# Two unused 32-byte tiles that move on-chip tiles by 32 and 64 bytes in a retention and two-mixture kernel

## Chip, cores and metric

The kernel runs on one core of a Trainium2 chip. The metric is the device time of one execution in microseconds (us), the median of several runs. Engines are called as the profile calls them: PE (TensorE matmuls) and PEld (its weight loads), DVE (VectorE), ACT (ScalarE), POOL (GpSimd) and SP (SyncE, which issues nearly all DMAs).

## What is computed

Three stages follow each other; the output of one is the input of the next.

```python
# 1: retention, B=4, H=8, S=576, D=64
scores = q @ k.T / sqrt(D)
x = (scores * Dmat) @ v                  # Dmat[i, j] = gamma**(i-j) for i >= j, else 0
x = x.transpose(0, 2, 1, 3).reshape(2304, 512)
# 2: routed mixture, 8 experts of 512 -> 1024 -> 512: each row goes to its best expert
e = argmax(x @ w_gate);  x = gate * (relu(x @ w1[e]) @ w2[e])
# 3: dense mixture: every row goes through all 8 experts
P = exp(logits - logits.max())
for _ in range(8):                       # Sinkhorn
    P /= P.sum(1) + 1e-9;  P /= P.sum(0) + 1e-9;  P *= N / E
out = sum(P[:, e:e+1] * (relu(x @ w1[e]) @ w2[e]) for e in range(8))
```

## The kernel before

**Precision.** A float32 operand is split into a high part (rounded to the type `fp32r`) and a low part (the rest). A product is then three matmuls: high by high, high by low, low by high. ACT makes the high part by a cast, DVE the low part by a subtraction (`lo_of`, L239 to L240).

**Stages on the clock.** Retention and routing take about the first 100 us, the routed mixture lasts until about 378 us, Sinkhorn runs beside the first unit of the dense mixture until about 412 us, and the dense mixture fills the rest. It goes over the 2304 rows in three passes (`NP = 3`) of 768 rows, and in each pass over 8 experts.

**Dense mixture, features.** The rows of a pass are held transposed, in four quarters of [128, 2, 384] float32 (tiles `x`, L1074). A Strassen-like scheme makes seven combinations of them (the quarters themselves, and sums and differences, one of which needs a tile of its own, `t3`), and each is split into a high tile `ch` and a low tile `cl` of [128, 2, 384] (L1099 and L1100). These fourteen tiles are called the features here. In passes 2 and 3 the same places are filled again at L1551 (the trace calls them `ch`, `cl` in pass 2 and `c` in pass 3).

**Dense mixture, pass 1** (about 378 to 850 us) is written out in order: `unit` (L1302) issues per quarter of an expert seven `product`s (L1313) with weights in the `ring` tiles. A product is six matmuls of 384 columns, L1318 to L1320, with the weights standing in PE and a feature tile streamed past them. `second` (L1236) multiplies the hidden rows in `HH` and `HL` by the second weights, also in `ring`, in matmuls of 512 columns (L1248 to L1250). The split first weights are stored to DRAM (`w1s`, L1306) for the passes to come.

**Dense mixture, passes 2 and 3** (about 850 us to the end) are placed by a planner: every piece of work is a `Task` with an engine, a cost in us and what it waits for; PE's order is a fixed line of tasks, and the order on the other engines comes from due times in a small simulation. The planner knows costs and buffers, not addresses. `first_weights` (L1564) loads the split first weights from `w1s` into one of five tiles `wa` (L1572), and `chunk` (L1606) issues the six matmuls of a product, L1622 to L1624:

```python
for r in range(2):
    a, b = (w[:, k, o + 128 * r:o + 128 * (r + 1)] for k in range(2))                     # of a tile wa
    nc.tensor.matmul(ps, a, xh[:, r, :], start=first, ...)                              # L1622
    nc.tensor.matmul(ps, a, xl_[:, r, :], start=False, ...)                              # L1623
    nc.tensor.matmul(ps, b, xh[:, r, :], start=False, ...)                              # L1624
```

The hidden rows go to nine tiles `hq` and four tiles `hr`, which are one stock of buffers: which of them a task gets depends only on which is free. They are combined by DVE (L1510, L1513) and split by ACT (L1729) and DVE (L240) into tiles `sq`; the second weights go through the `raw` tiles (and the two halves of `sums`) into tiles `wb`. `chunk2` multiplies them, L1779 to L1781 in matmuls of 256 columns and, in pass 3, L1776 and L1777. DVE adds the results to the accumulators `a0` to `a5` and `ya0` to `ya2` (L1802).

**Routed mixture.** `flipped` (L738) does the same three matmuls as a product, L741 to L743: the weights stand in PE, from `ring` tiles, and the routed rows (`HH`, `HL`) or the hidden rows (`h`) are streamed, up to 384 columns.

**Where tiles lie.** Tiles are taken from pools in the order in which the code asks for them. A pool with `side="right"` is laid out from the upper end of the on-chip memory, under the right pools that are open then. The first right pool is `sums` (L80), so that everything in a later right pool lies under it: the tiles of the retention stage (`io`, `wk`, `st`), then the features (`xc`), then the small tables of the dense mixture (`sk`, L1062), then the accumulators (`acc`), then `wa`, `hq` and three small buffers (`early`, L1377). Tiles of the left pools (`raw`, `ring`, `HH`, `HL`, `h`, `sq`, `wb`, `hr`, `ya`) don't depend on them.

Of the kernel before, what the change touches and what calls it, by code (L numbers as in the profile page):

```python
# [7 lines left out]
F32 = mybir.dt.float32  # L8
# [28 lines left out]
def kernel(  # L37
# [41 lines left out]
    ringt[:3] = [ring_p.tile([128, 4096], F32R, name=f"ring{i}") for i in range(3)]  # L79
    sum_p = ctx.enter_context(tc.tile_pool(name="sums", bufs=1, side="right"))  # L80
    sumt = sum_p.tile([128, 1024], F32, name="sums")

    xs = dram.tile([N + 1, DM], F32, name="xs")
    lst = dram.tile([LIST, 1], I32, name="lst")
# [12 lines left out]
    def bank(i, shape=(128, 512)):  # L97
        return psum.tile(list(shape), F32, tag=f"b{i}", name=f"b{i}")
# [121 lines left out]
    def tick(us):  # L220
        clock["pe"] += us
# [839 lines left out]
    sk = ctx.enter_context(tc.tile_pool(name="sk", bufs=1, side="right"))  # L1061
# [2 lines left out]
    TP = NT // NP  # L1064
    GRP = TP * 64
    HT = TP // 2
    P = sk.tile([128, NT, E], F32, name="P")
    lgall = sk.tile([128, NT, E], F32, name="lgall")

# [137 lines left out]
    def sinkhorn():  # L1207
# [8 lines left out]
        nc.vector.tensor_scalar(lgall, lgall, m, None, ALU.subtract)  # L1216
        nc.scalar.activation(P, lgall, AF.Exp)
        for it in range(8):
            nc.vector.tensor_reduce(rs, P, AX.X, ALU.add)
            nc.vector.tensor_scalar(rs, rs, 1e-9, None, ALU.add)  # L1220
            nc.vector.reciprocal(ri, rs)
            nc.vector.tensor_tensor(P, P, ri.unsqueeze(2).to_broadcast([128, NT, E]), ALU.mult)
            nc.vector.tensor_reduce(ce, P.rearrange("p t e -> p e t"), AX.X, ALU.add)
            o = bank((yield), (128, 128))
            nc.tensor.matmul(o[:, 0:E], ones, ce, start=True, stop=True)
            nc.vector.tensor_scalar(cr, o[:, 0:E], 1e-9, float(E) / N, ALU.add, ALU.mult)
            nc.vector.reciprocal(cr, cr)
            nc.vector.tensor_tensor(P, P, cr.unsqueeze(1).to_broadcast([128, NT, E]), ALU.mult)
    for _ in steps:
# [7 lines left out]
    def second(u, rows_, half_f, tiles_, last):  # L1237
# [3 lines left out]
        for t in tiles_:  # L1241
            tick(0.648)
            s = slice((t % HT) * 128, (t % HT + 1) * 128)
            first = u["i"] == 0 and not last
# [9 lines left out]
    def finish(p, e, t, y):  # L1254
        if e == 0:
            ACC[t] = acc_p.tile([128, DM], F32, name=f"a{t}")
        a = ACC[t]
        sc = P[:, p * TP + t, e:e + 1]
        if p == 0 and e == 0:
# [38 lines left out]

    A = tuple(range(HT))
    Bt = tuple(range(HT, TP))  # L1300
    def unit(u, pre, mids):
# [760 lines left out]
```

## Time and profile before

| | us |
|---|---|
| median of 3 runs | 1803.58 (1803.28 to 1805.52) |
| the profiled execution's own time | 1805.65 |
| its span, first to last instruction | 1803.9 |

| engine | busy, us | share of the span | instructions |
|---|---|---|---|
| PE | 1780.9 | 99% | 11996 |
| PEld | 1686.3 | 93% | 11996 |
| DVE | 1235.2 | 68% | 2246 |
| ACT | 856.5 | 47% | 1654 |
| POOL | 360.9 | 20% | 378 |

The profile comes from one execution, which took 2.07 us more than the median; 1.75 us of its time lie outside the span. Matmuls are pipelined, so the duration that the profile gives a matmul is longer than the time until the next one starts; what a matmul costs in a dense stretch is the distance from its start to the start of the next, its pitch.

### The profile page before, as it was taken

To read this page: it belongs to the slowest core of one execution; us is meant where nothing else is said; L and a number is where in the kernel's file an instruction comes from. 1 tells how busy PE (TensorE), PEld (TensorE's weight loads), DVE (VectorE), ACT (ScalarE), POOL (GpSimd) and SP (SyncE) were. 2 spreads that over 40 slices of the span, in tenths; PEclk is the share of its full clock that TensorE was granted. 3 is DMA by queue.
4 is the path that set the end of the run, shared out by engine and by line. 5 is a ranking of instruction groups with operands and counts; after the bars stand their busy time and mean duration, and the time that the engine had idled before them with its cause. 6 is when DMAs were issued, how large, how long until landed. Compare 5 with 4: busy or idle time off the path is not lost.

```text
span 1803.9 us, 31992 instructions
## 1 busy us (share of the span) xinstructions
PE 1780.9 (99%) x11996; PEld 1686.3 (93%) x11996; DVE 1235.2 (68%) x2246; ACT 856.5 (47%) x1654; POOL 360.9 (20%) x378
## 2 busy tenths in 40 slices
PE   9999999999999999999999999999999999999998
PEld 7889999988999999998999999999999999999998
DVE  6764666567655655664667787787877767787776
ACT  3554455534443434344565555555656544444442
POOL 6820121221321212213221112111222100000001
PEclk9999999999999999999999999999999999999999
DMA  9855655564545556545755888988785467888775
GB/s 307 293 187 167 207 178 185 206 201 154 210 164 196 189 191 228 191 162 192 228 155 179 280 283 293 308 291 286 262 285 184 124 204 245 255 252 246 256 228 187
DMA packets 200512, 398.64 MB, mean 221 GB/s; under 512 B 22278, under 2 KB 82839, under 8 KB 200348
## 3 DMA queue, kind: packets, MB, share of 16 engines
q1 hardware_dynamic: 197212, 386.56, 64.9%
q0 software_dynamic: 3136, 9.95, 1.5%
q8 instruction: 97, 1.59, 0.3%
q14 instruction: 67, 0.55, 0.1%
HBM read 278.93 MB, written 117.52 MB: 220 GB/s over the span
## 4 chain that ended last, share of the span: by engine, by line
PE 65%; issue 22%; DVE 3%; ACT 1%; DMA 1%; POOL 0%; POOLq 0%; ACTq 0%; DVEq 0%
PE b L1622 5%; PE b L1624 5%; PE b L1623 5%; PE b L1248 5%; PE b L1250 5%; PE b L1249 5%; PE b L1781 5%; PE b L1780 5%; PE b L1779 4%; PE b L1318 4%; PE b L1320 4%; PE b L1319 4%; PE b L741 4%; PE b L743 3%; PE b L742 3%
## 5 line engine op out<-in xcount | busy, mean ns | idle before, releaser
L1779 PE MATMUL b<-wb,sq 128*128 128x256 f32 x924 | 259.3, 281 | 0.8 <-DMA wb<-w2s 0.8
L1780 PE MATMUL b<-wb,sq 128*128 128x256 f32 x924 | 260.0, 281 | 0.0
L1781 PE MATMUL b<-wb,sq 128*128 128x256 f32 x924 | 259.4, 281 | 0.4 <-DVE sq L240 0.4
L240 DVE TENSOR_TENSOR ring<-raw,ring 128x512 fp32r<-128x512 f32 (+1 forms) x256 | 192.9, 762 | 67.1 <-ACT ring L263 58.7
L240 DVE TENSOR_TENSOR sq<-hq,sq 128x768 fp32r<-128x768 f32 x167 | 165.2, 993 | 67.4 <-ACT sq L1729 67.3
L1802 DVE SCALAR_TENSOR_TENSOR a<-b,P,a 128x256 f32<-128x256 f32 x327 | 151.1, 479 | 47.7 <-PE b L1781 24.0
L1781 PEld LDWEIGHTS b<-wb,sq 128*128 128x128 f32 x924 | 175.0, 189 | 0.6 <-DVE sq L240 0.6
L1779 PEld LDWEIGHTS b<-wb,sq 128*128 128x128 f32 x924 | 174.0, 188 | 1.2 <-issue 1.0
L1780 PEld LDWEIGHTS b<-wb,sq 128*128 128x128 f32 x924 | 174.7, 189 | 0.0
L1637 ACT ACTIVATE hq<-hq 128x384 f32<-128x384 f32 x144 | 75.7, 526 | 200.3 <-DVE hq L1634 199.9
L1729 ACT CAST sq<-hq 128x768 fp32r<-128x768 f32 x167 | 137.6, 829 | 39.7 <-PE b L1780 23.0
L1622 PE MATMUL b<-ch,wa 128*128 128x384 f32 x448 | 151.6, 338 | 2.2 <-DMA wa<-w1s 0.7
L1776 PE MATMUL b<-wb,sq 128*128 128x512 f32 x420 | 153.3, 397 | 0.0
L1318 PE MATMUL b<-ch,ring 128*128 128x384 f32 x448 | 152.5, 340 | 0.2
L1622 PE MATMUL b<-c,wa 128*128 128x384 f32 x448 | 151.1, 337 | 1.1 <-ACT u L1628 1.1
L1624 PE MATMUL b<-c,wa 128*128 128x384 f32 x448 | 150.9, 337 | 0.0
L1624 PE MATMUL b<-ch,wa 128*128 128x384 f32 x448 | 150.7, 336 | 0.0
L1623 PE MATMUL b<-c,wa 128*128 128x384 f32 x448 | 150.7, 336 | 0.0
L1319 PE MATMUL b<-cl,ring 128*128 128x384 f32 x448 | 150.6, 336 | 0.0
L1623 PE MATMUL b<-cl,wa 128*128 128x384 f32 x448 | 150.6, 336 | 0.0
L1320 PE MATMUL b<-ch,ring 128*128 128x384 f32 x448 | 150.6, 336 | 0.0
L1248 PE MATMUL b<-ring,HH 128*128 128x512 f32 x384 | 149.8, 390 | 0.0
(285 smaller groups left out, 4435.7 us busy)
## 6 DMA issues: line engine op xcount, KB each, us to landing
wa<-w1s SPq DMA_DIRECT2D x192, 512.0 KB, 4.8
raw<-in_moe_w_dram SPq DMA_DIRECT2D x128, 512.0 KB, 4.1
w1s<-ring SPq DMA_DIRECT2D x64, 896.0 KB, 5.9
w2s<-wb SPq DMA_DIRECT2D x84, 512.0 KB, 5.5
wb<-w2s SPq DMA_DIRECT2D x84, 512.0 KB, 4.5
raw<-in_moe_w_dram SPq DMA_DIRECT2D x66, 256.0 KB, 5.0
wa<-w1s SPq DMA_DIRECT2D x64, 256.0 KB, 5.9
kT<-in_kT_dram SPq DMA_DIRECT2D x18, 256.0 KB, 4.2
```

What stands on the lines that cost most here:

```text
L240: eng.tensor_tensor(lo, x, hi.bitcast(F32), ALU.subtract)
L1248: nc.tensor.matmul(y[t], hh[:, s], w.hi[:, f0:f0 + 512], start=first, stop=False)
L1318: nc.tensor.matmul(ps, a, xh[:, r, :], start=first and r == 0, stop=False, skip_group_check=True)
L1319: nc.tensor.matmul(ps, a, xl[:, r, :], start=False, stop=False, skip_group_check=True)
L1320: nc.tensor.matmul(ps, b, xh[:, r, :], start=False, stop=r == 1, skip_group_check=True)
L1622: nc.tensor.matmul(ps, a, xh[:, r, :], start=first, stop=False, skip_group_check=True)
L1623: nc.tensor.matmul(ps, a, xl_[:, r, :], start=False, stop=False, skip_group_check=True)
L1624: nc.tensor.matmul(ps, b, xh[:, r, :], start=False, stop=r == 1, skip_group_check=True)
L1776: nc.tensor.matmul(ps, hh[:, r, c], w[:, 512 * r:512 * (r + 1)], start=st, stop=end, skip_group_check=True)
L1779: nc.tensor.matmul(ps, hh[:, r, c], wh[:, r], start=st, stop=False, skip_group_check=True)
L1780: nc.tensor.matmul(ps, hh[:, r, c], wl[:, r], start=False, stop=False, skip_group_check=True)
L1781: nc.tensor.matmul(ps, hl[:, r, c], wh[:, r], start=False, stop=end, skip_group_check=True)
```

## The change

Two tiles are asked for that nothing writes or reads. Each takes 32 bytes per partition.

```diff
@@ -79,6 +79,7 @@
     sum_p = ctx.enter_context(tc.tile_pool(name="sums", bufs=1, side="right"))
     sumt = sum_p.tile([128, 1024], F32, name="sums")
+    sum_p.tile([128, 8], F32, name="edge")
 
@@ -1064,6 +1065,7 @@
     HT = TP // 2
+    sk.tile([128, 8], F32, name="step")
     P = sk.tile([128, NT, E], F32, name="P")
```

The first moves the tile `sums` and everything under it in the right pools down by 32 bytes, the second everything under it by 32 more. The start addresses in the two built programs, as the rest after division by 128 and by 256:

| tiles | moved by | modulo 128 | modulo 256 |
|---|---|---|---|
| features (`ch`, `cl`, `c`), their inputs `x`, `t3` | 32 | 96 to 64 | 224 to 192 |
| `sums` | 32 | 96 to 64 | 224 to 192 |
| retention: `qT`, `kT`, `k`, `v` | 32 | 96 to 64 | 224 to 192 |
| retention: `sc`, `cm`, `qdec` | 32 | 0 to 96 | 128 to 96 |
| retention: `sz`, `xT` | 32 | 32 to 0 | 160 to 128 |
| `P` | 32 | 64 to 32 | 64 to 32 |
| first weights of passes 2 and 3, `wa` | 64 | 64 to 0 | 64 to 0 |
| `hq`, `a0` to `a5` | 64 | 64 to 0 | 64 to 0 |
| `raw`, `ring`, `HH`, `HL`, `h`, `sq`, `wb`, `hr`, `ya` | 0 | 0 | 0 |

Within a tile, the two halves of a feature tile are 1536 bytes apart, and the pieces of 128 weights in `wa` 512 bytes; both are multiples of 256, so all pieces of a tile have the rest of its start. The two built programs have the same instructions in the same order on every engine and on every DMA queue, with the same waits.

## Rows read from the trace of the kernel before

**Rows 1.** The page: PE's granted clock in tenths, 40 slices of the span.
```profile
PEclk9999999999999999999999999999999999999999
```
**Rows 2.** Stretches: busy us and instructions by engine, clock, DMA share, GB/s.
```profile
412.00:850.00 438.00, 437.92 (x2210) 396.31 (x2208) 261.86 (x458) 177.61 (x370) 100.39 (x117) 1.00 0.52 187
850.00:1298.00 448.00, 445.76 (x3126) 443.62 (x3125) 332.68 (x499) 247.12 (x443) 89.62 (x68) 1.00 0.79 259
1315.00:1790.00 475.00, 474.58 (x2994) 455.16 (x2993) 359.68 (x582) 218.51 (x380) 32.69 (x32) 1.00 0.73 227
```
**Rows 3.** Groups by line and shape, PE: matmuls of 384 columns; busy us, mean ns, idle before.
```profile
L1318 PE MATMUL b<-ch,ring 128*128 128x384 f32 x448 | 152.5, 340 | 0.2
L1622 PE MATMUL b<-ch,wa 128*128 128x384 f32 x448 | 151.6, 338 | 2.2 <-DMA wa<-w1s 0.7 <-DVE hq L1634 0.6 <-ACT u L1628 0.6
L1622 PE MATMUL b<-c,wa 128*128 128x384 f32 x448 | 151.1, 337 | 1.1 <-ACT u L1628 1.1
L1624 PE MATMUL b<-ch,wa 128*128 128x384 f32 x448 | 150.7, 336 | 0.0
L1319 PE MATMUL b<-cl,ring 128*128 128x384 f32 x448 | 150.6, 336 | 0.0
L1623 PE MATMUL b<-cl,wa 128*128 128x384 f32 x448 | 150.6, 336 | 0.0
L1320 PE MATMUL b<-ch,ring 128*128 128x384 f32 x448 | 150.6, 336 | 0.0
L741 PE MATMUL b<-h,ring 128*128 128x384 f32 x32 | 11.1, 345 | 0.0
L742 PE MATMUL b<-h,ring 128*128 128x384 f32 x32 | 10.8, 338 | 0.0
L743 PE MATMUL b<-h,ring 128*128 128x384 f32 x32 | 10.7, 335 | 0.0
```
**Rows 4.** Timeline of PE in the routed mixture: start us, duration us, instruction.
```profile
116.41 0.33 PE L742 MATMUL b<-h,ring 128*128 128x384 f32 x1
...
117.62 0.34 PE L743 MATMUL b<-h,ring 128*128 128x384 f32 x1
```
**Rows 5.** Timeline of PE, pass 1: twelve matmuls of 384 columns and the next.
```profile
601.29 0.34 PE L1318 MATMUL b<-ch,ring 128*128 128x384 f32 x1
...
603.37 0.39 PE L1248 MATMUL b<-ring,HH 128*128 128x512 f32 x1
```
**Rows 6.** Timeline of PE, pass 2: six matmuls of 384 columns and the next.
```profile
908.89 0.34 PE L1622 MATMUL b<-ch,wa 128*128 128x384 f32 x1
...
909.93 0.28 PE L1779 MATMUL b<-wb,sq 128*128 128x256 f32 x1
```
**Rows 7.** Groups by line and shape, PE: retention matmuls of 128 columns.
```profile
L422 PE MATMUL b<-qT,kT 64*128 64x128 f32 x288 | 21.1, 286 | 2.6 <-DMA qT<-in_qT_dram 2.6
L491 PE MATMUL b<-sc,v 128*64 128x128 f32 x288 | 19.8, 281 | 0.0
```
**Rows 8.** One line's instructions, DVE: count, duration min/median/max ns, first and last start us.
```profile
L1510 DVE TENSOR_TENSOR hq<-hq,hq x65: 939/950/1643, 883.9 to 1774.1; 128x768 f32<-128x768 f32 x65
L1510 DVE TENSOR_TENSOR hr<-hr,hr x2: 957/958/958, 1121.6 to 1477.5; 128x768 f32<-128x768 f32 x2
```
**Rows 9.** Groups by line and shape, ACT: the same cast from tiles at either offset.
```profile
L1729 ACT CAST sq<-hq 128x768 fp32r<-128x768 f32 x167 | 137.6, 829 | 39.7 <-PE b L1780 23.0 <-PE b L1776 11.1 <-PE b L1781 1.7
L1729 ACT CAST sq<-hr 128x768 fp32r<-128x768 f32 x57 | 47.4, 832 | 27.5 <-PE b L1780 17.7 <-PE b L1776 9.2
```
**Rows 10.** DMA issues: count, KB each, median us from issue to landing.
```profile
wa<-w1s SPq DMA_DIRECT2D x192, 512.0 KB, 4.8
raw<-in_moe_w_dram SPq DMA_DIRECT2D x128, 512.0 KB, 4.1
```
**Rows 11.** The chain that ended last, 850 to 880 us: start us, us, what.
```profile
854.67 3.36 DMA wa<-w1s
...
868.39 5.81 DMA wa<-w1s
```

## The prediction

> **What bounds the kernel now.** I read the page's busy shares and clock first, then the stretches, then the groups by line, and last the timeline of PE at three places. The clock row shows 9 (90% or more) in every slice [rows 1], so no part of this time is PE at its lower level, and none can be given back by a faster clock. The stretches show the dense mixture: PE is busy for 437.92 of 438 us in pass 1, 445.76 of 448 in pass 2 and 474.58 of 475 in pass 3 [rows 2]. So from 412 us on the order of work hardly ever makes PE wait; the time is the number of matmuls times their pitch. A change that leaves every instruction and every wait where it was, as this one does, can only act in three ways: on the pitch of the matmuls that read a moved tile, on the few waits that are left (through a DMA, DVE, ACT or POOL that becomes faster or slower), or on the chains of the retention stage.
>
> How many matmuls read a moved tile, in the dense mixture: the nine groups L1318 to L1320 and L1622 to L1624 (in passes 2 and 3 apart), each of 448 [rows 3], so 9 x 448 = 4032 stream a feature tile (offset 96 modulo 128, then 64), and 6 x 448 = 2688 of these also load their weights from `wa` (64, then 0). Everything else on PE there (L1248 to L1250, L1776 to L1781) reads tiles that do not move.
>
> **Features on PE: 0.** The trace of before holds its own control. The routed mixture streams 384 columns from `h` with weights from `ring`, both at 0 modulo 128; pass 1 streams 384 columns from the features at 96 with weights at 0; passes 2 and 3 stream the features at 96 with weights at 64. The pitches are: (117.62 - 116.41) / 7 = 172.9 ns [rows 4], (603.37 - 601.29) / 12 = 173.3 ns [rows 5], (909.93 - 908.89) / 6 = 173.3 ns [rows 6]. The timeline is rounded to 10 ns, so each has an uncertainty of 1 to 2 ns. The durations are finer: 345, 338, 335 ns for the aligned triple, 340, 336, 336 for pass 1 and 338, 336, 336 for pass 2 [rows 3]. The first of a triple also carries short stalls, so the last of the three is the cleanest: 335 against 336 and 336. If the features at 64 did all that tiles at 0 do, the gain would be 1 ns x 4032 = 4.0 us; taking the last matmul of the triple for all nine groups is the most favourable reading. The other end, from the whole triples: 1018 ns aligned against 1012 in pass 1, so 2 ns slower each, which is mostly the first matmul's stalls. I take 0, because the row nearest to the new state is the old one: 96 and 64 are both off a multiple of 128, and even a tile that is on it has the same pitch.
>
> **Weights on PE: 0.** Pass 1 against pass 2 is the control for `wa`: features at 96 in both, weights at 0 against 64. 340 + 336 + 336 = 1012 against 338 + 336 + 336 = 1010 [rows 3]. So weights at 0 come out 2 / 3 = 0.7 ns slower, which on 2688 matmuls is 1.8 us of loss; the second and third matmul of the triple show no difference at all. I take 0 and keep +1.8 as an end; the other end is in the 4.0 us above.
>
> **DVE, ACT and POOL: 0.** `hq` (64) and `hr` (0) are one stock of buffers, so the same instruction stands in the trace at both offsets: a DVE sum over 768 columns takes 950 ns at the median all in `hq` (65 of them) and 958 ns all in `hr` (2) [rows 8], and an ACT cast takes 829 ns from `hq` and 832 ns from `hr` [rows 9]. With `hq` at 0 afterwards these stay within 1% of what they are; what differs between such groups elsewhere is who runs beside them. Cover: PE is at 99.5% or more in passes 2 and 3, and waits for DVE or ACT just ahead of L1622 for 0.6 + 0.6 + 1.1 = 2.3 us [rows 3]; even a gain of the whole would stay under 0.2%.
>
> **DMAs into `wa`: 0, at most -2.0.** 192 transfers of 512 KB land in 4.8 us at the median at offset 64, and the 128 of 512 KB into `raw`, at 0, in 4.1 [rows 10]; the two run in stretches with DMA shares of 0.73 to 0.79 and of 0.52 (most `raw` loads fall in pass 1 and before) [rows 2], so load explains the difference as well as the offset does. Suppose it were all offset, 0.7 / 4.8 = 15% of a transfer. Then the single PE wait put down to such a DMA, 0.7 us [rows 3], would go, and the two stretches in which the chain runs through one, 3.36 and 5.81 us [rows 11], would shrink by 15% of 9.17 = 1.4 us, of which PE's other work hides most. Together at most 2.1 us, rounded to 2.0 since they overlap. I take 0: elsewhere the transfers are issued ahead, and PE does not wait for them.
>
> The Trainium skill (DMA: Bandwidth & Descriptors, section How a descriptor splits into AXI transactions) says that a descriptor which does not start on a 256-byte boundary is cut into one transaction more, the first one partly unused. By that rule a 2048-byte piece of a row of `wa` at 64 costs 66 beats of 32 bytes and 64 after the change, an estimate of 3% of each such transfer; the section speaks of reads, and here it is the written side that moves. By the rule the sum would be 3% of the 9.17 us, about -0.3 us, instead of 0, and no row here separates it from the load.
>
> **Retention: 0, at most +1.4.** Here tiles move both ways: `qT` and `kT` from 96 to 64, `sc`, `cm` and `qdec` from 0 to 96. The matmuls that read `qT` at 96 take 286 ns, those that read `sc` at 0 take 281 [rows 7]. They differ in rows and columns of the array too, so 5 ns is a bound: 288 x 5 ns = 1.4 us if all of L491 lost it. The unused tiles themselves cost no instruction, and PE's order and DVE's are the same as before.
>
> **Sum.** 0 on the profiled execution's own time of 1805.65 us. That execution lies 2.07 us above the median, so for the median I forecast 1803.58 + 0, **1803.6 us**. Ends of the costs: 4.0 + 2.0 = 6.0 us down, 1.8 + 1.4 = 3.2 us up.
>
> **The rivals.**
>
> 1. *Features read in pieces of 64 bytes (faster).* A row of 384 float32 is 1536 bytes: 24 such pieces from offset 64, but 25 from 96, where it starts in the middle of a piece. If PE paid for pieces, one in 25 of the pitch of 173.3 ns, 6.9 ns, would go on 4032 matmuls: 28 us, 1775.7. For it: PE is the bound, so all of a gain on the pitch counts. Against it: the aligned `h` tiles should then already show a pitch some 7 ns shorter, and they show 172.9 against 173.3 [rows 4 to 6]. What the rows leave of it is the 1 ns from above, 1799.6 us. It would count as faster by 0.2% from 0.9 ns per matmul on.
>
> 2. *Engines meet in the same place (slower).* Before the change, `wa` and `hq` lie at 64 while `sq`, `wb`, `raw` and `hr` lie at 0; afterwards all of these start at 0 modulo 128. If simultaneous accesses at the same offset hinder each other, PE's weight loads would now meet DVE's and ACT's accesses, as in the routed mixture, where weights and both operands are at 0. There a triple takes 1018 ns against 1010 in pass 2 [rows 3], 2.7 ns per matmul more: 2688 x 2.7 = 7.2 us, so 1810.8 us. For it: that row. Against it: pass 1 also has weights, `HH` and `HL` at 0, and it stands at 1012 with the same pitch; and the 345 is the first matmul alone. It decides from 3.6 us / 2688 = 1.3 ns per matmul on.
>
> 3. *The change does not do what it says.* Both tiles could be rounded away or fall into a gap. The start addresses in the built programs speak against it, and the time would be 1803.6 as well, so it has no share of its own.
>
> **How the numbers follow.** A measurement of this kernel can tell about 0.2% from no change, 3.6 us: faster means under 1800.0, slower over 1807.2. My forecast, no change (the DMA term and the rule of the skill included, since 2.0 us stay within it), has 0.79: three controls for PE and two for the other engines say so. Rival 1 in its small form has 0.11, rival 2 has 0.10. The range from 1798.5 to 1808.0 holds the upper end of the costs, 1803.6 + 3.2 = 1806.8, and the small form of rival 1, 1799.6, with 1 us more on each side for the spread of the runs (their highest is 1805.52); it leaves out the far end down, 1797.6, which needs every favourable reading at once, and rival 2 at full price.
>
> **What would show it.** Right: L1318 to L1320 and L1622 to L1624 keep 336 to 340 ns and a pitch of 173 ns; the sums in `hq` stay at 945 to 960 ns; `wa` lands in 4.6 to 5.0 us; PE's busy time stays within 3 us of 1780.9. Rival 1 would show as a shorter pitch in pass 1 already, where only the features move; rival 2 as a longer pitch in passes 2 and 3 alone, with pass 1 unchanged. If PE's pitch is unchanged and the time is not, a wait must have appeared or gone, and the idle time ahead of L1622 would say which. The forecast is wrong if the pitch of the 4032 matmuls moves by 1 ns or more either way.

## The result and the profile after

| | before | after |
|---|---|---|
| median, us (6 runs each) | 1803.43 (1800.95 to 1805.52) | 1813.45 (1812.35 to 1814.68) |
| the profiled execution: its time and its span | 1805.65, 1803.9 | 1813.11, 1811.3 |

The ratio is 1.0056, with an interval of 1.0043 to 1.0069: **10.0 us slower**, and above the range that ended at 1808.0.

The page of the changed kernel, its span, busy times and clock:

```profile
span 1811.3 us, 31992 instructions
...
PE 1789.5 (99%) x11996; PEld 1696.9 (94%) x11996; DVE 1235.3 (68%) x2246; ACT 858.3 (47%) x1654; POOL 361.7 (20%) x378
...
PEclk9999999999999999999999999999999999999999
```

The instructions are the same in number, and the clock is granted everywhere as before [rows 1]. PE is busy for 8.6 us more, DVE for 0.1 us more. The stretches of [rows 2], in the changed kernel:

```profile
412.00:850.00 438.00, 437.92 (x2197) 396.99 (x2196) 260.73 (x452) 175.92 (x365) 99.85 (x115) 1.00 0.51 185
850.00:1298.00 448.00, 445.91 (x3089) 444.15 (x3088) 326.77 (x493) 244.95 (x438) 89.39 (x69) 1.00 0.78 257
1315.00:1790.00 475.00, 474.29 (x2966) 455.54 (x2965) 358.91 (x582) 219.27 (x382) 29.65 (x29) 1.00 0.72 225
```

PE is as busy as before to 0.3 us in every stretch, but does less in it: 2197 matmuls against 2210, 3089 against 3126, 2966 against 2994. So no wait has come in; each matmul takes longer. The groups by line and shape (every line after the second tile's lies two further down, so L1318 to L1320 are now L1320 to L1322, and L1622 to L1624 are L1624 to L1626):

```profile
L1320 PE MATMUL b<-ch,ring 128*128 128x384 f32 x448 | 152.7, 341 | 0.1
L1624 PE MATMUL b<-ch,wa 128*128 128x384 f32 x448 | 152.7, 341 | 2.1 <-DVE hq L1636 1.5 <-ACT u L1630 0.6
L1625 PE MATMUL b<-cl,wa 128*128 128x384 f32 x448 | 152.3, 340 | 0.0
L1624 PE MATMUL b<-c,wa 128*128 128x384 f32 x448 | 151.9, 339 | 0.6 <-ACT u L1630 0.6
L1626 PE MATMUL b<-ch,wa 128*128 128x384 f32 x448 | 151.4, 338 | 0.0
L1322 PE MATMUL b<-ch,ring 128*128 128x384 f32 x448 | 151.4, 338 | 0.0
L1250 PE MATMUL b<-ring,HH 128*128 128x512 f32 x384 | 149.7, 390 | 0.0
```

Against [rows 3] the mean durations are up by 1 to 4 ns, in pass 1 too; L1250, which reads no moved tile, stands at 390 as it did before, then as L1248:

```profile
L1248 PE MATMUL b<-ring,HH 128*128 128x512 f32 x384 | 149.8, 390 | 0.0
```

How much time that is can't be read off these modelled durations. It can be read off one line's instructions (count, duration min/median/max ns, first and last start in us): within a pass the distance from the first start to the last is the length of the pass. Before:

```profile
L1318 PE MATMUL b<-ch,ring x448: 334/336/445, 334.3 to 838.2; 128*128 128x384 f32 x150
L1622 PE MATMUL b<-ch,wa x448: 336/336/444, 838.7 to 1291.5; 128*128 128x384 f32 x150
L1622 PE MATMUL b<-c,wa x448: 334/336/448, 1292.7 to 1764.9; 128*128 128x384 f32 x150
```

and after:

```profile
L1320 PE MATMUL b<-ch,ring x448: 333/338/443, 331.9 to 839.4; 128*128 128x384 f32 x150
L1624 PE MATMUL b<-ch,wa x448: 332/338/446, 840.0 to 1297.6; 128*128 128x384 f32 x150
L1624 PE MATMUL b<-c,wa x448: 333/338/442, 1298.8 to 1772.8; 128*128 128x384 f32 x150
```

The passes took 503.9, 452.8 and 472.2 us, and now take 507.5, 457.6 and 474.0: **+3.6, +4.8 and +1.8, together +10.2 us**. Ahead of pass 1 this execution is 2.4 us earlier (331.9 against 334.3), which differs from execution to execution (332.1 and 335.7 in two kernels below whose first 300 us have the addresses of before); that is why the spans differ by 7.4 us alone.

The timeline of PE at the places of [rows 5] and [rows 6], twelve matmuls of 384 columns in pass 1 and six in pass 2, each with the instruction that follows:

```profile
600.94 0.34 PE L1320 MATMUL b<-ch,ring 128*128 128x384 f32 x1
...
603.06 0.39 PE L1250 MATMUL b<-ring,HH 128*128 128x512 f32 x1
...
914.04 0.34 PE L1624 MATMUL b<-ch,wa 128*128 128x384 f32 x1
...
915.11 0.27 PE L1781 MATMUL b<-wb,sq 128*128 128x256 f32 x1
```

(603.06 - 600.94) / 12 = 176.7 ns, where it was 173.3, and (915.11 - 914.04) / 6 = 178.3, where it was 173.3. Over a whole pass the mean pitch (from each start of such a matmul to the next start; a distance is left out as a gap where it is over 30 ns longer than the columns take at 2.4 GHz, the granted clock) rose from 174.0 to 176.4 ns in pass 1, from 173.7 to 177.9 in pass 2 and from 174.0 to 176.6 in pass 3. Summed over all matmuls of the passes, the unmoved ones too, the longer pitch is 3.4 + 5.8 + 2.4 = 11.6 us; what the gaps left out take beyond their columns shrank by 1.3 us (from 11.2 to 9.9). Together that is the 10.2 us to 0.1 us.

DVE's sums (L1510, now L1512) have not changed, 951 ns at the median against 950 [rows 8]:

```profile
L1512 DVE TENSOR_TENSOR hq<-hq,hq x65: 942/951/1652, 885.2 to 1782.0; 128x768 f32<-128x768 f32 x65
```

### The profile page after: what moved, and what is told of

It is laid out like the page before. It is cut to its first block, busy times and chain, and to the rows that moved or that the text cites. A ratio compares the mean times of both kernels' runs of the same rounds, so it can differ in the third digit from the quotient of the medians.

```text
span 1811.3 us, 31992 instructions
## 1 busy us (share of the span) xinstructions
PE 1789.5 (99%) x11996; PEld 1696.9 (94%) x11996; DVE 1235.3 (68%) x2246; ACT 858.3 (47%) x1654; POOL 361.7 (20%) x378
## 4 chain that ended last, share of the span: by engine, by line
PE 66%; issue 22%; DVE 3%; ACT 1%; DMA 0%; POOL 0%; POOLq 0%; ACTq 0%; DVEq 0%
PE b L1624 5%; PE b L1625 5%; PE b L1626 5%; PE b L1250 5%; PE b L1251 5%; PE b L1252 5%; PE b L1783 5%; PE b L1782 5%; PE b L1781 4%; PE b L1320 4%; PE b L1321 4%; PE b L1322 4%; PE b L742 4%; PE b L744 3%; PE b L743 3%
## 5 line engine op out<-in xcount | busy, mean ns | idle before, releaser
L1783 PEld LDWEIGHTS b<-wb,sq 128*128 128x128 f32 x924 | 175.2, 190 | 0.6 <-DVE sq L241 0.6
L1781 PEld LDWEIGHTS b<-wb,sq 128*128 128x128 f32 x924 | 174.6, 189 | 0.7 <-issue 0.6
L1782 PEld LDWEIGHTS b<-wb,sq 128*128 128x128 f32 x924 | 174.8, 189 | 0.0
L1624 PE MATMUL b<-ch,wa 128*128 128x384 f32 x448 | 152.7, 341 | 2.1 <-DVE hq L1636 1.5
L1320 PE MATMUL b<-ch,ring 128*128 128x384 f32 x448 | 152.7, 341 | 0.1
L1624 PE MATMUL b<-c,wa 128*128 128x384 f32 x448 | 151.9, 339 | 0.6 <-ACT u L1630 0.6
L1626 PE MATMUL b<-ch,wa 128*128 128x384 f32 x448 | 151.4, 338 | 0.0
L1322 PE MATMUL b<-ch,ring 128*128 128x384 f32 x448 | 151.4, 338 | 0.0
L1626 PE MATMUL b<-c,wa 128*128 128x384 f32 x448 | 151.1, 337 | 0.0
L1250 PE MATMUL b<-ring,HH 128*128 128x512 f32 x384 | 149.7, 390 | 0.0
```

Of the source, the lines that this page charges most:

```text
L1250: nc.tensor.matmul(y[t], hh[:, s], w.hi[:, f0:f0 + 512], start=first, stop=False)
L1320: nc.tensor.matmul(ps, a, xh[:, r, :], start=first and r == 0, stop=False, skip_group_check=True)
L1322: nc.tensor.matmul(ps, b, xh[:, r, :], start=False, stop=r == 1, skip_group_check=True)
L1624: nc.tensor.matmul(ps, a, xh[:, r, :], start=first, stop=False, skip_group_check=True)
L1626: nc.tensor.matmul(ps, b, xh[:, r, :], start=False, stop=r == 1, skip_group_check=True)
L1781: nc.tensor.matmul(ps, hh[:, r, c], wh[:, r], start=st, stop=False, skip_group_check=True)
```

## The experiments

Four theories were tried, as they came up; the letters are those of the recorded expectations. First (F), that the **features' own offset** counts. Second (W), that **weights at offset 0** are slow in themselves. Third (C), the prediction's second rival, that **other engines** meet PE in the same place. Fourth (R), formed from the result, that the **pair** counts: the distance, modulo 256, from the start of the weights to the start of the streamed tile. Two more stand beside it in the expectations: that each pair of offsets has a value of its own (B), and that the matmuls before count as well (H). "X matmuls" are there the 384-column matmuls that stream a feature tile, and a value such as 13.3 ns is a pitch above the 160 ns that 384 columns take at 2.4 GHz. Each experiment is read by the three passes and by the pitch of their 384-column matmuls, as above. Offsets are modulo 256, `ring` is at 0. The kernel before ran beside each; in the runs repeated for their times its median lay between 1802.96 and 1803.83. The first tile of the change stands below the pool `sums`, the second in `sk`; where a diff shows one size alone, that tile alone is there.

### The parts of the change

**Features alone moved as in the change (192), `wa` and `hq` left in place.**

```diff
+    sum_p.tile([128, 8], F32, name="edge")
+    sk.tile([128, 56], F32, name="step")
```

> Only the features (with the sums tile and the retention tiles) move, from 96 to 64 modulo 128 (224 to 192 modulo 256); the first weights wa, hq and the accumulators stay at 64 modulo 256. Theory F (the offset of the streamed tile alone sets the pitch: at 64 each matmul that streams a feature tile costs 2 to 3 ns more, whatever the weights): pitch of the 4032 matmuls up by 2 to 3 ns in all three passes, time 1811 to 1814 us. Theory W (passes 2 and 3 became slower because their weights moved to 0): pass 1 slower by about 3.3 us as in the change, passes 2 and 3 as before, 1805.5 to 1808 us. Theory R (what counts is the distance between streamed tile and weights, modulo 256: 192 is bad; 0, 160 and 224 are not): pass 1 slower by 3.3 us, passes 2 and 3 at a distance of 128 that no run has shown.

Measured: 1810.91 us, 1.0041 (1.0028 to 1.0055). Passes 506.8, 455.6, 473.2; pitches 176.4, 176.0, 175.5 ns. Moving the features alone costs +2.9, +2.8 and +1.0 us.

**`wa`, `hq` and the accumulators alone moved (0), features left at 224.**

```diff
+    sk.tile([128, 16], F32, name="step")
```

> Only wa, hq, the accumulators and the small tables move, by 64 bytes (wa from 64 to 0 modulo 128); the features stay at 96. Theory F: no change, 1802 to 1805 us, all pitches at 173.3 ns. Theory W: pass 1 as before, passes 2 and 3 slower by 1.3 to 3.5 ns per matmul on 2688, 1807 to 1812 us. Theory R: distance 224 as in pass 1 before, so no change, 1802 to 1805 us.

Measured: 1809.92 us, 1.0038 (1.0024 to 1.0051). Passes 503.6, 457.1, 473.7; pitches 173.9, 175.8, 175.6 ns. Pass 1 is that of before, passes 2 and 3 lose 4.3 and 1.5 us. So features that stay where they were stream more slowly past weights that moved. None of the three theories with an expectation here had both of these runs: F expected no change in this one, R none either (distance 224, as in pass 1 before), and W, which holds here, expected passes 2 and 3 of the one before it to stay.

**`wa` alone at 0**, `hq` and the accumulators back at 64 by a gap:

```diff
+    wa_ = new("wa", 5, 1024, F32R)
+    new("gap", 1, 16)
-        "w1": [two(x) for x in new("wa", 5, 1024, F32R)],
+        "w1": [two(x) for x in wa_],
```

> Only wa moves, from 64 to 0; a gap of 64 bytes behind it keeps hq, the accumulators, the small tables and the features where they were. Theory W (weights at 0): the whole of the loss of the run in which wa, hq and the accumulators moved, +5 to +7 us, 1809 to 1811. Rival C (hq and the accumulators at the same offset as the tiles they are combined with hinder PE): no change, 1802 to 1805. Theory R: distance 224, at which pass 1 before stood at 14 ns, so no change either, 1802 to 1805.

**`hq` and the accumulators alone at 0**, `wa` at 64:

```diff
+    sk.tile([128, 16], F32, name="step")
...
+    wa_ = new("wa", 5, 1024, F32R)
+    new("gap", 1, 48)
-        "w1": [two(x) for x in new("wa", 5, 1024, F32R)],
+        "w1": [two(x) for x in wa_],
```

> The other half of that run: hq and the accumulators move from 64 to 0, wa and the features stay. Theory W: no change, 1802 to 1805 us. Rival C: +5 to +7 us, 1809 to 1811, with pitches of L1622 to L1624 and of L1779 to L1781 1 to 2 ns longer though no matmul operand moved. If both this run and the one before lose about half, both count.

Measured: 1809.58 us, 1.0033 (1.002 to 1.0045), and 1803.74 us, 1.0003 (0.9994 to 1.0012). Pass 2, one line's instructions, with `wa` alone at 0:

```profile
L1624 PE MATMUL b<-ch,wa x448: 336/337/445, 836.4 to 1293.3; 128*128 128x384 f32 x150
```

and with `hq` and the accumulators alone at 0:

```profile
L1625 PE MATMUL b<-ch,wa x448: 336/336/452, 839.9 to 1292.1; 128*128 128x384 f32 x150
```

456.9 us and 452.2, where before it was 452.8. The whole loss is in `wa`; `hq` and the accumulators meeting others at 0 cost nothing, which ends the third theory for DVE's and ACT's tiles; for `wa` meeting the others at 0 the runs with features 64 and `wa` 0 and with PE alone, below, end it. W held again, and R missed, since it expected no change from `wa` alone and the time rose by 6.5 us: passes 2 and 3 now have the pair of pass 1 (features at 224, weights at 0), and take 175.8 and 175.6 ns where pass 1 takes 174.0. The mean pitches of passes 1 to 3 agree with those of the kernel with the same addresses on PE (the one above, and before) within 0.06 ns: they are set by addresses and are not noise.

**The first tile alone** (features 192, `wa` 32):

```diff
+    sum_p.tile([128, 8], F32, name="edge")
```

> The first of the two unused tiles alone: features from 224 to 192 modulo 256, wa (and hq, the accumulators) from 64 to 32, so the distance between them stays 160. Pass 1 as with the change, 16.4 ns above columns / 2.4 GHz, under every theory (+3.3 us). Theory R (the distance modulo 256 decides): passes 2 and 3 as before, 13.7 and 14.0 ns, so 1806 to 1808 us. Theory F: as in the run that moved the features alone, 16 and 15.5 ns, 1810 to 1812. Theory B (each pair of offsets has its own value and no simple distance rule holds): 1804 to 1816.

**The second tile alone** (features 224, `wa` 32):

```diff
+    sk.tile([128, 8], F32, name="step")
```

> The second unused tile alone: features stay at 224 modulo 256, wa (and hq, the accumulators) from 64 to 32, distance 192. Pass 1 as before, 13.96 ns. Theory R: passes 2 and 3 at 16 to 18 ns as other pairs at a distance of 192, +6 to +10 us, 1810 to 1814. Theory F: no change, 1802 to 1805. Theory B: between.

Measured: 1807.36 us, 1.0026 (1.0014 to 1.0037), passes 506.9, 453.0, 471.4, pitches 176.5, 174.0, 174.5; and 1807.15 us, 1.0019 (1.001 to 1.0028), passes 503.7, 455.5, 472.5, pitches 173.9, 176.1, 175.2. The first tile alone lengthens only pass 1. The pair theory's figure for it held. Its figure for the second tile was too high, though the sign was right: the distance is 192 there as in the change, and pass 2 lost 2.7 us instead of 4.8.

### Which offsets are slow

**Features at 128 and at 160, `wa` left at 64:**

```diff
+    sum_p.tile([128, 24], F32, name="edge")
+    sk.tile([128, 40], F32, name="step")
```

> The features move from 96 to 0 modulo 128 (224 to 128 modulo 256), wa, hq and the accumulators stay at 64 modulo 256. Theory F with 64 alone as the bad offset: pitch and time as before, 1802 to 1805 us, as the tiles h of the routed mixture at 0 suggest. If instead every multiple of 64 is bad for the features: 1811 to 1814 us. Theory W: 1802 to 1805 us. Theory R: distances 128 in pass 1 and 64 in passes 2 and 3, both not seen so far.

```diff
+    sum_p.tile([128, 16], F32, name="edge")
+    sk.tile([128, 48], F32, name="step")
```

> The features move from 96 to 32 modulo 128 (224 to 160 modulo 256), wa, hq and the accumulators stay at 64 modulo 256. Theory F: as 96, an odd multiple of 32: pitch and time as before, 1802 to 1805 us; if the pitch falls with the offset instead, 32 would lie between 0 and 64. Theory W: 1802 to 1805 us. Theory R: distance 160 in pass 1 and 96 in passes 2 and 3; 160 was not slow in pass 2 before, so pass 1 as before.

Measured: 1807.59 us, 1.0022 (1.0013 to 1.0031), pitches 175.5, 174.2, 174.0; and 1815.69 us, 1.0067 (1.0053 to 1.008), pitches 173.8, 176.8, 176.2. Neither the theory of the features' offset nor W expected either loss; R had expected pass 1 of the second to stay as before. The second of these is slow in another place as well: its pass 1 is 4.0 us longer although its features stream at the pitch of before. The groups of pass 1 (412 to 830 us) that read unmoved tiles alone, with features at 160:

```profile
L1252 PE MATMUL b<-ring,HL 128*128 128x512 f32 x320 | 126.8, 396 | 0.0
...
L1251 PE MATMUL b<-ring,HH 128*128 128x512 f32 x319 | 126.0, 395 | 0.0
```

and before:

```profile
L1249 PE MATMUL b<-ring,HH 128*128 128x512 f32 x324 | 126.0, 389 | 0.0
L1250 PE MATMUL b<-ring,HL 128*128 128x512 f32 x323 | 125.7, 389 | 0.0
```

Two of the three groups of 512 columns with `ring`, `HH` and `HL`, none of which moved, go from 389 to 396 and 395 ns, the mean pitch of all three from 227.3 to 231.5. Only the matmuls between which they stand read a moved tile. So what a matmul costs also hangs on those before it.

**Features at seven different offsets at once** (0, 32, up to 192, by unused pads), `wa` at 64 and, in a second kernel, at 0:

```diff
+    sum_p.tile([128, 8], F32, name="edge")
+    sk.tile([128, 8], F32, name="step")
...
+        if i and i not in XC:
+            xc_p.tile([128, 8], F32, name=f"pad{i}")
```

> Pads of 32 bytes between the feature tiles put the seven combinations at seven offsets, 0, 32, 64, 96, 128, 160, 192 modulo 256, with the ring weights of pass 1 at 0 and wa at 64, as before. Read: the pitch above columns / 2.4 GHz of each combination. Theory R (the distance of the streamed tile from the weights, modulo 256, sets it; by the runs so far about 13.3 ns at 0, 14 at 64, 16.8 at 96, 15.7 at 128, 13.8 at 160, 16.4 to 18 at 192, 14 at 224): pass 1 shows these in the order of the offsets, and passes 2 and 3 show them shifted by 64, so the combination at 64 is at 13.3 there and the one at 0 at 16.4 or more. Theory F (the streamed tile's offset alone): the same value for a combination in pass 1 and in passes 2 and 3; 64 and 192 bad in both. A third theory, H (the state left by the matmuls before it counts more than the offset): no such order, since neighbours now differ.

```diff
-    sk.tile([128, 8], F32, name="step")
+    sk.tile([128, 24], F32, name="step")
```

> As the run before, but wa, hq and the accumulators at 0 modulo 256. Theory R: passes 2 and 3 now show the same value per combination as pass 1. Theory F: passes 2 and 3 as in the run before, the weights don't count. Pass 1 as in the run before under every theory, since nothing of it moved.

Measured, one run each: 1815.65 us and 1812.68. In pass 1, whose addresses are the same in both, the pitch by feature offset is 176.3, 176.5, 172.4, 177.0, 175.3, 173.1, 175.6 ns for 0 to 192 (172.4 for 64), the same in both kernels within 0.13 ns. In pass 2 the offset 64, at 176.9, is the slowest with `wa` at 64, and the fastest, 173.5, with `wa` at 0. No offset of the features is good or bad by itself, which ends the first theory. R fared no better as a full rule: with `wa` at 0, where it expected the values of pass 1 in passes 2 and 3, the offset 192 took 178.1 and 176.3 ns there against 175.7 in pass 1.

### The pair

**Other pairs: features 160 with `wa` 0, and 64 with 0.** The second has all the remainders of the change modulo 128.

```diff
+    sum_p.tile([128, 16], F32, name="edge")
```

> Features and wa move by the same 64 bytes, 224 to 160 and 64 to 0 modulo 256; distance 160 as before. Pass 1 as in the run with the features at 160: 13.8 ns there, but the matmuls of 512 columns beside them at 18.2 ns (+5 us). Theory R: passes 2 and 3 as before, 13.7 and 14.0 ns, so about 1808 to 1810 us. Theory W (weights at 0 are bad by themselves): 15.8 and 15.6 ns, 1813 to 1817.

```diff
+    sum_p.tile([128, 40], F32, name="edge")
+    sk.tile([128, 40], F32, name="step")
```

> Features at 64 and wa at 0 modulo 256: modulo 128 the same offsets as the change has, modulo 256 not. In the map the combination at 64 had the shortest pitches of all with weights at 0, 12.4 ns in pass 1 and 13.5 to 13.7 in passes 2 and 3. If the pair modulo 256 decides: X matmuls at 12.4 to 13.7 ns, 1800 to 1804 us, unless the matmuls of 512 columns beside them become slower. If modulo 128 decides: as the change, 1812 to 1815. If the state left by the neighbours decides, the map's value need not hold when all seven combinations stand at 64.

Measured: 1812.86 us, 1.0049 (1.0034 to 1.0063), passes 507.8, 456.2, 472.7; and 1803.7 us, 1.0002 (0.9993 to 1.0011), passes 504.7, 453.8, 470.5. The first lies between the theories: the distance is that of before, but its pitches in passes 2 and 3 are 175.1 and 175.3 ns, where R had 173.7 and 174.0 and W 175.8 and 175.6, and its time is above R's 1808 to 1810 us. Its unmoved 512-column matmuls lose as with features at 160 above. With 64 and 0 the pitches are 173.4, 173.6 and 173.7, shorter than before in each pass. Pass 2 in that kernel:

```profile
L1624 PE MATMUL b<-ch,wa x448: 332/336/446, 837.5 to 1291.3; 128*128 128x384 f32 x150
```

453.8 us with `wa` at 0, against 457.6 in the changed kernel with the same remainders modulo 128. That ends the second theory, and with it the count modulo 128 in which the prediction was made. What the 384-column matmuls gain is given back by others whose tiles stayed in place: the 512-column ones of pass 1 take 228.6 ns against 227.3, and the 256-column ones of passes 2 and 3 take 118.9 against 118.2.

**PE alone.** This kernel leaves out the whole computation. It runs 24 matmuls of 384 columns for each of 16 x 8 pairs of offsets, four `product`s of one pair on end, first with the weights' offset in the outer loop, then with the streamed tile's:

```diff
+    for w in range(0, 256, 32):
+        for m in range(0, 512, 32):
+            for _ in range(4):
+                product(m, w)
+    for m in range(0, 512, 32):
+        for w in range(0, 256, 32):
+            for _ in range(4):
+                product(m, w)
```

> The disputed cost by itself: the whole computation is left out (the output is a constant), and PE alone runs products of six 384-column matmuls like L1622 to L1624, for 16 offsets of the streamed tile (0 to 480 modulo 512) by 8 offsets of the weights (0 to 224 modulo 256), four products a pair, in two orders of the pairs. No other engine and no DMA runs beside it. Theory R (distance modulo 256): all pairs at the same distance have the same pitch, and the same in both orders; 64 and 160 short, 96, 128 and 192 long. Theory F: the value follows the streamed tile's offset alone. Theory B: each pair its own value, the same in both orders. Theory H: the two orders differ for the same pair. If the pitch is the same for all pairs here, the cost needs other engines' accesses beside PE.

Its one stretch, 10 to 1090 us (columns as in the stretches above):

```profile
10.00:1090.00 1080.00, 1080.00 (x6172) 1080.00 (x6170) 0.00 (x0) 0.32 (x1) 0.00 (x0) 1.00 0.01 2
```

DVE and POOL do nothing and DMA moves 2 GB/s, so whatever differs between pairs is PE's own. The timeline, each time the first of the last 18 of a pair's 24 matmuls and the matmul that follows them, for the pairs (streamed, weights) of (64, 0), (96, 0) and (224, 64) in the first order. These are addresses modulo 256, as everywhere here; the tiles `mv` and `wt` of this kernel themselves start at 128, so that its loops reach (64, 0) as `product(448, 128)`:

```profile
346.28 0.34 PE L73 MATMUL ps<-mv,wt 128*128 128x384 f32 x1
...
349.40 0.34 PE L73 MATMUL ps<-mv,wt 128*128 128x384 f32 x1
...
350.45 0.34 PE L73 MATMUL ps<-mv,wt 128*128 128x384 f32 x1
...
353.64 0.34 PE L73 MATMUL ps<-mv,wt 128*128 128x384 f32 x1
...
434.39 0.34 PE L73 MATMUL ps<-mv,wt 128*128 128x384 f32 x1
...
437.57 0.34 PE L73 MATMUL ps<-mv,wt 128*128 128x384 f32 x1
```

and (224, 64) in the second order:

```profile
681.97 0.34 PE L73 MATMUL ps<-mv,wt 128*128 128x384 f32 x1
...
685.09 0.34 PE L73 MATMUL ps<-mv,wt 128*128 128x384 f32 x1
```

These are 173.3, 177.2 and 176.7 ns, and 173.3 in the second order. The same pair takes 176.7 or 173.3 by what ran before it. The median pitch of the sixteen pairs at each distance (over the last 18 matmuls of a pair), with what the passes of the other kernels show in which all features have one offset (14 kernels of three passes, the changed one and the kernel before among them, and those of the last two experiments below):

| distance, streamed minus weights, modulo 256 | PE alone, first / second order, ns | in the passes, ns |
|---|---|---|
| 0 | 173.4 / 173.4 | 173.7 to 175.5 |
| 32 | 173.4 / 176.7 | not tried |
| 64 | 173.4 / 173.7 | 173.3 to 174.2 |
| 96 | 176.8 / 176.6 | 176.2 to 176.8 |
| 128 | 176.2 / 176.2 | 175.5 to 176.0 |
| 160 | 176.7 / 173.4 | 173.7 to 175.3 |
| 192 | 174.8 / 174.6 | 175.2 to 177.9 |
| 224 | 173.6 / 173.6 | 173.9 to 175.8 |

With PE alone the pitch hangs on the distance and not on either offset by itself, and a streamed tile at m and at m + 256 does the same, at every distance but 32 and 160. 64 is short and 96 and 128 are long both here and in the passes. At 32 and 160 the order decides, for all but one or two of the sixteen pairs. The kernel before had 224 in pass 1 (174.0) and 160 in passes 2 and 3 (173.7 and 174.0); the change made all three 192 (176.4, 177.9, 176.6).

**Distance 0: both at 0, and both at 64** (with `ring` at 0, pass 1 then has 0 and 64).

```diff
+    sum_p.tile([128, 56], F32, name="edge")
+    sk.tile([128, 24], F32, name="step")
```

> Features, wa, hq and the accumulators all at 0 modulo 256: distance 0 in all three passes, at which the runs of PE alone show 13.3 to 13.4 ns in either order. Theory R: X matmuls at 13.3 to 13.6 ns (before 13.96, 13.69, 14.02), a gain of 1.5 to 2.5 us, 1801 to 1802.5 us. Theory H (what the matmuls before leave behind decides as well): X matmuls as R says, but the matmuls of 512 and 256 columns between them may take up to 1.5 ns more, +1 to +4 us, so 1802 to 1806.

```diff
+    sum_p.tile([128, 40], F32, name="edge")
+    sk.tile([128, 24], F32, name="step")
```

> Features and wa both at 64 modulo 256: distance 64 in pass 1 and 0 in passes 2 and 3. Theory R: X matmuls at 13.4 ns in pass 1 (as measured with the features at 64) and 13.3 to 13.6 in passes 2 and 3; matmuls of 512 columns in pass 1 at 15.3 as in that run (+1.6 us). 1802 to 1804.5 us. Theory W (weights at 0 bad, at 64 good): the same; the two theories part in the run at 0 and 0, where W expects passes 2 and 3 at 15.6 to 15.8.

Measured: 1807.86 us, 1.0027 (1.0016 to 1.0038), passes 509.7, 453.6, 469.7, pitches 175.5, 174.1, 173.7; and 1806.03 us, 1.001 (1.0001 to 1.002), passes 504.2, 453.5, 472.5, pitches 173.3, 174.0, 174.7. Both were expected faster than that. With both at 0 pass 3 is the shortest of all (its 512-column matmuls on `wb` and `sq`, which did not move, take 229.8 ns against 234.4 before), and pass 1 the longest: distance 0 costs 2.1 ns more there than with PE alone, and the unmoved 512-column matmuls go to 231.3. Its first line shows at the same time how little the durations tell:

```profile
L1320 PE MATMUL b<-ch,ring x448: 332/334/447, 333.1 to 842.8; 128*128 128x384 f32 x150
```

The median duration is 2 ns below that of before, and the pass is 5.8 us longer.

No arrangement beat the kernel before; 64 with 0 equals it.

## Why the prediction was wrong

**What bounds the kernel** stood: PE is busy throughout, the instructions and waits are the same, and the pitch is what changed, on the 4032 matmuls that were named. That the other matmuls would keep theirs did not hold to the end: those of 512 columns in pass 3 went from 234.4 to 232.3 ns, 0.9 us in all. By the bound that the prediction set itself (1 ns or more either way) its forecast is wrong: +2.4, +4.2 and +2.6 ns in passes 1 to 3.

**Features on PE: 0** is the step that failed. It held [rows 4] (streamed 0, weights 0), [rows 5] (96 and 0) and [rows 6] (96 and 64) to be controls, and took "the row nearest to the new state" to be the old one. Modulo 256 the three rows are distances of 0, 224 and 160, and all happened to be short: 172.9, 173.3 and 173.3 ns. None had the new distance, 192. Three equal rows showed that these pairs are alike, and not that offsets don't matter. With the features alone moved, passes 1 to 3 grew by 2.9, 2.8 and 1.0 us where the term was 0. The only loss in sight, 2 ns on the whole triples, had been put down to stalls and kept out of the range; on 4032 matmuls it would have been 8.1 us, but it belonged to another pair, so its size is chance.

**Weights on PE: 0, at most +1.8** failed for the same reason, and its bound was too low: `wa` alone cost 4.1 and 1.7 us in passes 2 and 3. Pass 1 against pass 2 compared weights at 0 with weights at 64 past the same features, but that changes the distance from 224 to 160, and says nothing of 192. Pass 1 could not have priced pass 2 in any case: with `wa` alone at 0 both have the pair (224, 0), at 174.0 and 175.8 ns. Each operand was weighed alone, so no pair had a price, and the two prices do not add: features alone and `wa` alone cost 2.8 + 4.1 us in pass 2, both together 4.8.

**The durations** on which the small bounds were built (345, 338, 335 and the like) are modelled and don't measure the pitch, as the kernel with both at 0 shows.

**DVE, ACT and POOL: 0** held: 951 ns against 950, and `hq` and the accumulators alone at 0 gave 1.0003.

**DMAs into `wa`: 0** could not be told apart from so small a sum. The idle time ahead of the first matmul of a product no longer names a DMA (0.7 us before [rows 3]), but the pass is longer all the same. In the kernel with `wa`, `hq` and the accumulators alone at 0 the 192 transfers land in 4.7 us at the median, against 4.8 at 64, so the difference of 0.7 us from the transfers into `raw` was not the offset. The estimate of -0.3 us by the rule on descriptors of the Trainium skill (DMA: Bandwidth & Descriptors, section How a descriptor splits into AXI transactions) is below what these runs resolve.

**Retention: 0** stands within the spread: pass 1 began at 331.9 us, and at 332.1 and 335.7 in kernels with the addresses of before.

**Rival 1** had the sign wrong: pass 1, where only the features move, became slower. **Rival 2** had the right sign and nearly the time (1810.8 against 1813.45), but by chance, since its mechanism is one that the runs exclude: pass 1 lengthened too, `hq` at 0 costs nothing, `wa` at 0 is fast with features at 64 (173.6 ns in pass 2), and PE shows the cost with the other engines at rest. The Trainium skill (SBUF — State Buffer, section Who interferes with whom) states that PE never waits on anyone, in a list of which engine hinders which. The runs agree as far as the tiles of the other engines go (1.0003 with `hq` and the accumulators at 0); what they add is that PE's time depends on where its own two operands lie.

**What is shown and what stays open.** Shown: the loss is in the pitch; it needs no other engine; and it comes from where the streamed tile and the weights start, neither of them by itself. With PE alone the distance modulo 256 sets the pitch at six of the eight distances. In the whole kernel it is not enough, and three things speak against a pure rule of distance there: 192 costs from 175.2 to 177.9 ns in the passes and 174.7 with PE alone; the pair (224, 0) takes 174.0 ns in pass 1 and 175.8 in pass 2; and where the features lay at seven offsets with `wa` at 64, distance 192 (offset 0) was short at 173.5 and distance 0 (offset 64) long at 176.9. The matmuls before count in part. In pass 2 of the changed kernel the six matmuls of a product that stands between matmuls of other tiles take, in order, 180.9, 182.2, 175.8, 177.4, 175.8 and 177.4 ns on the mean, where before they took 174.9, 173.2, 173.8, 173.4, 173.3 and 173.4: the loss is largest in the two that follow the other tiles, and stays at 2 to 4 ns after them. Why the distance counts, and what of the past is carried over, was not found. A price for one pair, from PE alone, would have given the change the right sign in pass 1 (174.8 against 173.6) and too little of it, and no sign in passes 2 and 3, where the old distance of 160 took 176.7 or 173.4 by the order.

## What to carry to other kernels

In this kernel, where PE has no idle time, the start addresses of a matmul's two operands are part of its cost: with 4000 matmuls, 2.5 ns on each are 10 us, and two tiles of 32 bytes that nobody uses did it (each alone cost some 3.5 us). A row can be a control for a new address only if it has the new pair, both operands together and modulo 256, and the same matmuls around it; equal pitches at other pairs prove nothing, and even the same pair took 1.8 ns more in another pass. After any edit that shifts a pool, read the pitch from start to start in the timeline, in each pass and also for matmuls whose tiles did not move.

## What was not expected of the hardware

- With PE alone at the full granted clock, a 384-column matmul with new weights takes from 173.4 to 176.8 ns at the median by the distance of its operands, and two distances have both a short and a long value, by what ran before.
- Matmuls whose own tiles stay in place change by 4 ns and more when the tiles of their neighbours move: those of 512 columns with `ring` go from 227.3 to 231.5 (features at 160) and 231.3 (both at 0), and those of pass 3 on `wb` and `sq` become shorter, from 234.4 to 232.3 in the changed kernel and to 229.8 with both at 0.
- The pitch is reproducible: kernels with the same addresses on PE agree within 0.06 ns in the mean of a pass, while their whole times spread by 2 us and more.
